# Softmax weights applied after the value product, and values, phi(keys) and retrieved values turned by VectorE and DMA instead of TensorE

## The chip, the core and the metric

The kernel runs on one core of a Trainium2 chip. Its engines each work through a queue of their own, in order: TensorE (PE in the profile; PEld is its weight load), VectorE (DVE), ScalarE (ACT), GpSimd (POOL) and SyncE (SP), which issues nearly all DMAs here. An instruction that waits holds up what stands behind it on its engine, and a DMA that waits for an earlier one holds up every DMA behind it in the queue of SP. The metric is the device time of one launch in microseconds (us). Before the change it is 2301.6 us, the median of three runs (2299.87 to 2302.35).

## The reference

One transformer layer over 2048 tokens of width 1024. The first half is an attention with a compressive memory: 32 heads of width 32, the tokens in four segments of 512. The second half is a layer norm and an MLP of inner width 3584. In the attention, for every head and segment `s`:

```python
logits = einsum("qd,kd->qk", qs, ks) * scale + mask   # causal inside the segment
p      = softmax(logits)
a_dot  = p @ vs
a_mem  = (phi(qs) @ M) / (phi(qs) @ z + 1e-6)         # phi(t) = t+1 if t>0 else exp(t)
o      = g * a_mem + (1 - g) * a_dot                  # g = sigmoid(beta), one number a head
M, z   = M + phi(ks).T @ vs,  z + sum(phi(ks))
```

Then `h = x + o @ wo`, and `h + MLP(LN(LN(h)))`. All is float32. The matrix products of the kernel split an operand into a high and a low part (`fp32r`) and add three products.

## The kernel before

The four segments are taken in two halves of two. In each half come an attention stage (about 40 to 500 us and 885 to 1375 us), the product with `wo`, and the MLP stages. Only the attention and its edges are touched by the change.

**Units.** Eight groups `g` of four heads times the two segments of the half make 16 units in a half, 32 in all. In half 0 they are segments 0 and 1, in half 1 segments 2 and 3. `dense` computes keys, queries and values of one unit: eight steps each for `kps`, `qps` and `vps`, three 128x512 matmuls a step, with the result laid out as 128 rows (4 heads x 32) by 512 tokens. Meanwhile `heads` runs the softmax of the unit before it, one step of `heads` after one step of `dense` (`interleave`).

**A head's pipeline.** `slot` runs six steps for a head after the list `PLAN`. In it three heads are under way: the current one (`q`: logits, row minimum, exponential), the one before (`n`: normalise; `t`: turn the weights so that keys lie on partitions; `s`: their low part) and the one before that (`a`: product with the values; `o`: into the output tile `ot`). Before the change `norm` multiplies all weights, 128 rows by up to 512, by the inverse of their row sum and by `1 - g`. It does so on POOL, after one reciprocal on DVE (L554, L557).

**What is turned.** Three things come with head dimensions on partitions and are needed with tokens on partitions, or the other way. These are the values (`vt` into `vn`, L469), phi of the keys (`pk` into `pkn`, L453; not in the last segment, which updates no memory), and what is retrieved from the memory (`om` into `pom`, L516; not in the first segment, which has none). Each is four 128x128 transposes on PE, with `ident` as the moving operand. ACT then writes the high part, or the copy, and DVE the low part.

**Late work.** The generator `late` of a unit is run during the next `dense`. It turns the values, queues small matmuls (`pm`: retrieval; `pmm`: memory update), which go out one at a time between the heads' matmuls (`one_small`), and turns what was retrieved.

**The queue of SP.** In each unit it carries 12 DMAs of 64 KB that stack keys (`ks`, L377), 12 that stack queries (`qs`, L377), the output tile to memory (`o_dram`, L609) and the loads of the next weights (`wr`, L326). The next unit's logits wait for `ks` and `qs`. A scheduler sets the order on each engine; only the instructions of some later stages are held to the order written.

**After the attention.** The last unit's heads run beside the first `wo` blocks (`wo_first`), which take the tiles `zx_tile(.., 3)` of the pool `zt` for a part of the weights.

Of the kernel before, what the change touches and what calls it, by code (L numbers as in the profile page):

```python
# [17 lines left out]
P = 128  # L18
S = 2048
# [11 lines left out]
PLAN = ('q1 S2', 'q0 n0 a0', 'q2 t0 a1', 'q3 n2 s0 o', 't1', 's1 t2')  # L31
# [12 lines left out]
def build(tc, x, wq, wk, wv, wo, beta, w1, b1, w2, b2, out):  # L44
# [39 lines left out]

    acts = {}
# [258 lines left out]
    def attention(half, first):  # L344
# [6 lines left out]

        def tmpr(name):
            return ab.tile([P, 512], F32R, tag="tmpr", name=name, bufs=6)
# [48 lines left out]
        def dense(g, sl, ws, u):  # L402
# [30 lines left out]
            for c in project(ws["v"], sl, "vps", vps):  # L433
# [16 lines left out]
                if c == 1 and s < 3:  # L450
                    pkn = ps_dense("pkn")
                    for i in range(4):
                        nc.tensor.transpose(pkn[:, i * P:(i + 1) * P], pk[:, i * P:(i + 1) * P], ident)  # L453
# [12 lines left out]
            def late():  # L466
                vn = ps_dense("vn")
                for c in range(4):
                    nc.tensor.transpose(vn[:, c * P:(c + 1) * P], vt[:, c * P:(c + 1) * P], ident)  # L469
                vn3 = vn.rearrange("p (a b) -> p a b", b=DH)  # L470
                nc.scalar.copy(vs[:, :, 0:32], vn3)
                nc.vector.tensor_tensor(vs[:, :, 32:64], vn3, raw(vs[:, :, 0:32]), op=ALU.subtract)
                yield
                if s > 0:
# [14 lines left out]
                    for i2 in range(2):  # L489
                        smalls("pm", [(lambda ps, ii=ii: ps[:, 256 * ii:256 * ii + 132],  # L490
                                       pqh[:, (2 * i2 + ii) * P:(2 * i2 + ii + 1) * P],
                                       pql[:, (2 * i2 + ii) * P:(2 * i2 + ii + 1) * P], mzh, mzl, True, True)
                                      for ii in range(2)], partial(memory, i2))
                left = len(small)
                if s < 3:
                    def update(pmm):
# [9 lines left out]
                                    vs[:, 4 * c:4 * c + 4, 0:32], vs[:, 4 * c:4 * c + 4, 32:64], c == 0, c == 3)  # L506
# [5 lines left out]
                if s > 0:  # L512
                    pom = ps_dense("pom")
                    for i in range(4):
                        one_small()
                        nc.tensor.transpose(pom[:, i * P:(i + 1) * P], om[:, i * P:(i + 1) * P], ident)  # L516
                    if s == 3:
                        yield
                        while acts["pth"][0] < 2:
                            yield  # L520
                    op = nc.scalar.copy(omt, pom)
                    if s == 3:
                        tc.add_manual_dep(op.ins, acts["pth"][1].ins.name, NOSYNC, reason="program order")
# [9 lines left out]
        def qk(st, i):  # L533
            u, j = st["u"], st["j"]
            if "pr" not in st:
                st["pr"] = ab.tile([P, 1280], F32, name="pr", bufs=2)
                st["mx"] = ab.tile([P, 32], F32, name="mx", bufs=4)
                st["nm"] = ab.tile([P, 32], F32, name="nm", bufs=4)
# [13 lines left out]
        def norm(st, i):  # L552
            pr, mx, nm, j, g = st["pr"], st["mx"], st["nm"], st["j"], st["u"]["g"]
            nc.vector.reciprocal(nm[:, 4 + i:6 + i], mx[:, 4 + i:6 + i])  # L554
            for k in (i, i + 1):
                pi = pr[:, offs[k]:offs[k] + P * (k + 1)]
                nc.gpsimd.tensor_scalar(pi, pi, nm[:, 4 + k:5 + k], gate[:, 1, 4 * g + j:4 * g + j + 1],  # L557
                                        op0=ALU.mult, op1=ALU.mult)
# [23 lines left out]
        def av(st, n):  # L582
# [4 lines left out]
            for jk in (0, 1) if n == 0 else (3, 2):  # L587
                w = 512 - P * jk
                v = u["vs"][:, 4 * jk + j, :]
# [10 lines left out]
        def av_out(st):  # L600
# [4 lines left out]
            if j == 3:  # L605
                if u["omt"] is not None:
                    nc.gpsimd.tensor_tensor(ot, ot, u["omt"], op=ALU.add)
# [8 lines left out]
        def slot(cur):  # L616
# [6 lines left out]
            ops = {"q": (cur, qk), "n": (cur, norm), "N": (p1, norm), "t": (p1, ptr), "s": (p1, sub), "S": (p2, sub),  # L623
# [820 lines left out]
```

## Time and profile before

| what | value |
|---|---|
| median of the runs | 2301.6 us |
| profiled execution, first to last instruction | 2296.2 us |
| granted TensorE clock | 1.000 |
| PE busy | 2270.4 us (99%) |
| PEld busy | 1890.8 us (82%) |
| DVE busy | 1540.3 us (67%) |
| ACT busy | 1225.0 us (53%) |
| POOL busy | 1092.4 us (48%) |

The page gives for each engine the time in which it was busy. A matmul's duration includes its way through the array, so consecutive matmuls overlap: what one costs in an unbroken run is the distance from its start to the next start, its pitch, and not its duration. Groups of instructions are listed by line and tile, with their count and mean duration, and waits are put down to the instruction that released them. For a DMA there are two numbers: how long SP was busy issuing it, and the time from its issue until its data had landed.

### The profile page before, as it was taken

The numbers are of one execution on the slowest core, as the hardware profiler recorded it, in microseconds if no ns is written. First come the engines' busy times: TensorE is split into PE (matmuls) and PEld (weight loads), VectorE is DVE, ScalarE is ACT, GpSimd is POOL, SyncE is SP. The second block draws the span as 40 slices with busy tenths as digits, with TensorE's granted clock in tenths as the row PEclk, the third lists the DMA queues.
The fourth block names the chain that finished last, engine by engine and source line by source line (L and its number), as shares of the span: only waits on it lengthen the run. The fifth ranks groups of instructions, "written<-read, shape, count | busy, mean of one in ns | idle before, by whom it ended". The sixth has DMA issues, their size and how long they took to land.

```text
span 2296.2 us, 35279 instructions
## 1 busy us (share of the span) xinstructions
PE 2270.4 (99%) x11769; PEld 1890.8 (82%) x11769; DVE 1540.3 (67%) x3173; ACT 1225.0 (53%) x2549; POOL 1092.4 (48%) x1134
## 2 busy tenths in 40 slices
PE   8999999999999999999999999999999999999999
PEld 6888888878888888888888887888888888888887
DVE  6777777776655565777777777565566766577563
ACT  6777777775453445777777776363344223322221
POOL 5545555555244442555555556253445554155430
PEclk9999999999999999999999999999999999999999
DMA  6333333345465654433333344466667976476762
GB/s 190 92 85 91 93 89 85 87 120 182 139 204 172 188 165 142 113 91 86 85 87 88 87 111 140 156 211 175 176 188 263 345 243 216 159 253 221 249 234 90
DMA packets 322719, 355.36 MB, mean 155 GB/s; under 512 B 26190, under 2 KB 218730, under 8 KB 322538
## 3 DMA queue, kind: packets, MB, share of 16 engines
q1 hardware_dynamic: 259370, 316.40, 45.4%
q10 hardware_dynamic: 63168, 36.71, 5.3%
q8 instruction: 93, 1.52, 0.3%
q14 instruction: 88, 0.72, 0.1%
HBM read 226.59 MB, written 76.09 MB: 132 GB/s over the span
## 4 chain that ended last, share of the span: by engine, by line
PE 91%; ACT 3%; POOL 2%; DVE 2%; issue 1%; DMA 1%; ACTq 0%; SPq 0%; POOLq 0%; DVEq 0%
PE po L1278 22%; PE bps L882 9%; PE cps L882 7%; PE dps L882 6%; PE po L593 6%; PE ppt L573 6%; PE pqk L541 3%; PE vps L116 2%; PE vps L115 2%; PE kps L115 2%; PE kps L116 2%; PE vps L117 2%; PE kps L117 2%; PE pwo L117 2%; PE pwo L116 2%; PE pwo L115 2%
## 5 line engine op out<-in xcount | busy, mean ns | idle before, releaser
L557 POOL TENSOR_SCALAR pr<-pr,nm,gate 128x128 f32<-128x128 f32 (+3 forms) x512 | 322.6, 639 | 345.9 <-DVE nm L554 260.0
L550 ACT ACTIVATE pr<-pr,mx 128x256 f32<-128x256 f32 (+3 forms) x512 | 287.6, 562 | 161.9 <-DVE mx L542 158.2
L580 DVE TENSOR_TENSOR ptl<-ppt,pth 128x512 fp32r<-128x512 f32 (+1 forms) x384 | 227.2, 599 | 86.2 <-ACT pth L575 82.0
L542 DVE CUSTOM_DVE_ANT_0 pr<-pqk,mask 128x256 f32<-128x256 f32 (+3 forms) x512 | 243.3, 484 | 46.5 <-PE pqk L541 43.7
L573 PE MATMUL ppt<-ident,pr 128*128 128x128 f32 x1280 | 223.6, 277 | 2.1 <-POOL pr L557 1.4
L575 ACT CAST pth<-ppt 128x512 fp32r<-128x512 f32 (+1 forms) x384 | 194.2, 517 | 39.0 <-PE ppt L573 33.1
L1288 DVE TENSOR_TENSOR c<-c,po 128x512 f32<-128x512 f32 x160 | 105.4, 683 | 143.1 <-PE po L1278 135.5
L573 PEld LDWEIGHTS ppt<-ident,pr 128*128 128x128 f32 x1280 | 164.6, 140 | 32.5 <-POOL pr L557 2.6
L541 PE MATMUL pqk<-ks,qs 96*128 96x256 f32 (+3 forms) x512 | 161.3, 315 | 0.0
L92 POOL TENSOR_TENSOR wl<-wr,wh 128x1024 fp32r<-128x1024 f32 x52 | 124.5, 2393 | 70.8 <-PE pqk L541 27.6
L593 PE MATMUL po<-pth,vs 128*64 128x512 f32 (+3 forms) x512 | 155.4, 326 | 0.3 <-ACT pth L575 0.2
L593 PE MATMUL po<-ptl,vs 128*64 128x512 f32 (+3 forms) x512 | 153.9, 310 | 1.3 <-DVE ptl L580 1.2
L1278 PE MATMUL po<-w2h,zh 128*128 128x512 f32 x378 | 121.1, 390 | 0.8 <-DVE zh L1218 0.4
L1135 POOL TENSOR_TENSOR w2r<-w2r 128x512 f32<-128x512 f32 x54 | 85.4, 1593 | 72.0 <-DVE c L1288 36.9
L541 PEld LDWEIGHTS pqk<-ks,qs 96*128 96x128 f32 x512 | 96.2, 188 | 21.5
L994 POOL TENSOR_TENSOR s<-r 128x512 f32<-128x512 f32 x28 | 43.6, 1559 | 143.4 <-DVE sa L1010 87.1
L882 PE MATMUL bps<-zh,sb 128*128 128x512 f32 x336 | 111.0, 391 | 0.0
L882 PE MATMUL bps<-zh,sa 128*128 128x512 f32 x336 | 110.8, 390 | 0.0
L115 PE MATMUL vps<-yh,wh 128*128 128x512 f32 x256 | 109.4, 427 | 0.9 <-DVE MZ L497 0.9
L115 PE MATMUL kps<-yh,wh 128*128 128x512 f32 (+1 forms) x264 | 110.1, 417 | 0.0
L115 PE MATMUL qps<-yh,wh 128*128 128x512 f32 x256 | 106.8, 417 | 0.0
L1278 PE MATMUL po<-w2h,hl 128*128 128x512 f32 x322 | 103.2, 390 | 0.5 <-POOL hl L1218 0.3
(241 smaller groups left out, 6657.1 us busy)
## 6 DMA issues: line engine op xcount, KB each, us to landing
hr<-h_dram SPq DMA_DIRECT2D x112, 448.0 KB, 5.4
w2r<-in_B_w SPq DMA_DIRECT2D x122, 256.0 KB, 4.4
r<-in_B_w SPq DMA_DIRECT2D x56, 512.0 KB, 4.5
h_dram<-ht ACTq DMA_DIRECT2D x84, 256.0 KB, 3.7
ks<-kh SPq DMA_DIRECT2D x256, 64.0 KB, 2.0
qs<-qh SPq DMA_DIRECT2D x256, 64.0 KB, 2.0
wr<-in_A_wo SPq DMA_DIRECT2D x32, 512.0 KB, 4.0
wx<-in_B_w SPq DMA_DIRECT2D x56, 256.0 KB, 3.5
```

Of the source, the lines that this page charges most:

```text
L115: nc.tensor.matmul(ps, ah, bh, start=first, stop=False)
L116: nc.tensor.matmul(ps, ah, bl, start=False, stop=False)
L541: nc.tensor.matmul(pqk[:, :n], u["qs"][j][:, i * P:(i + 1) * P], u["ks"][j][:, 0:n], start=True, stop=True)
L542: nc.vector.tensor_tensor_reduce(out=st["pr"][:, offs[i]:offs[i] + n], in0=pqk[:, :n], in1=mask[:, 512 - n:512], op0=ALU.add, op1=ALU.min, ...
L550: nc.scalar.activation(pi, pi, AF.Exp, bias=mx[:, i:i + 1], scale=-1.0, accum_out=mx[:, 4 + i:5 + i])
L557: nc.gpsimd.tensor_scalar(pi, pi, nm[:, 4 + k:5 + k], gate[:, 1, 4 * g + j:4 * g + j + 1], op0=ALU.mult, op1=ALU.mult)
L573: nc.tensor.transpose(ppt[:, o:o + P], pr[:, offs[i] + jk * P:offs[i] + (jk + 1) * P], ident)
L575: acts["pth"] = n, nc.scalar.copy(pth[:, base:base + w], ppt[:, :w])
L580: nc.vector.tensor_tensor(o, x0, x1, op=ALU.subtract)
L593: nc.tensor.matmul(po[:, P * jk:], v, st[part][:, koff[jk]:koff[jk] + w], start=(jk, part) == (0, "pth"), stop=(jk, part) == (2, "ptl"))
L882: nc.tensor.matmul(ps, x_[:, c, :], y_[:, c, :], start=first and c == 0 and n == 0, stop=last and c == 3 and n == 2, skip_group_check=True)
L1278: nc.tensor.matmul(ps, x_[:, k], y_[k], start=opens and k == 0 and i == 0, stop=closes and k == self.KP - 1 and i == 2, skip_group_check=True)
```

## The change

The softmax weights are no longer normalised before they are turned. `norm` and its tiles are gone. `inverse` takes the four row sums of a head at once into a tile `rs`; after the fourth head POOL multiplies them by `1 - g`. `weigh` turns this 128x16 tile with one transpose on PE, copies it, writes it to memory and reads it back with each row repeated over the 32 partitions of its head. The result `w` multiplies the whole output tile on POOL in `av_out`.

The three turns leave PE. `turned` transposes 32x32 blocks on DVE, writes the tile to memory, and reads it back with four DMAs, one for each 32 partitions. So keys and tokens inside a unit come in another order, and the operands of `pmm`, `av` and `av_out` are indexed to fit. The values' halves (`vs`) are now made in `late` after the retrieval's matmuls are queued and six more steps have passed. The low part of phi(keys) moves from DVE to POOL.

```diff
-PLAN = ('q1 S2', 'q0 n0 a0', 'q2 t0 a1', 'q3 n2 s0 o', 't1', 's1 t2')
+PLAN = ('q1 r S2', 'q0 a0', 'q2 t0 w a1', 'q3 s0 o', 't1', 's1 t2')
...
+        scr = [acts["zt"].tile([P, 4, 512], F32, tag=f"t{x_}3", name=f"sc{x_}") for x_ in "hl"]
+        def turned(src, to, mid):
+            nc.vector.transpose(mid.rearrange("p (c k d) -> p c k d", c=4, k=4), src.rearrange("p (k c d) -> p c k d", c=4, k=4))
+            d = turn_dram[acts.get("turned", 0) % len(turn_dram)]
+            acts["turned"] = acts.get("turned", 0) + 1
+            nc.sync.dma_start(d, mid)
+            for c in range(4):
+                nc.sync.dma_start(to[32 * c:32 * c + 32].rearrange("j (h x) -> j h x", h=4),
+                                  d[:, c * P:(c + 1) * P].rearrange("(h j) x -> j h x", h=4))
...
+                if c == 3 and s < 3:
+                    kn = scr[1][:, 2 + sl]
+                    turned(pk, kn, scr[1][:, 0])
...
-                    pkn = ps_dense("pkn")
-                    for i in range(4):
-                        nc.tensor.transpose(pkn[:, i * P:(i + 1) * P], pk[:, i * P:(i + 1) * P], ident)
-                    nc.scalar.copy(pkh, pkn)
-                if c == 2 and s < 3:
-                    nc.vector.tensor_tensor(pkl, pkn, raw(pkh), op=ALU.subtract)
+                    pkn = kn.rearrange("p (h k d) -> p k h d", h=4, k=4)
+                    nc.scalar.copy(pk4[0], pkn)
+                if c == 3 and s < 3:
+                    nc.gpsimd.tensor_tensor(pk4[1], pkn, raw(pk4[0]), op=ALU.subtract)
...
-            vt = tmp("vt")
-            nc.scalar.copy(vt, vps)
+            vn = scr[0][:, 2 + sl]
+            turned(vps, vn, scr[0][:, 0])
...
-                vn = ps_dense("vn")
-                for c in range(4):
-                    nc.tensor.transpose(vn[:, c * P:(c + 1) * P], vt[:, c * P:(c + 1) * P], ident)
-                vn3 = vn.rearrange("p (a b) -> p a b", b=DH)
-                nc.scalar.copy(vs[:, :, 0:32], vn3)
-                nc.vector.tensor_tensor(vs[:, :, 32:64], vn3, raw(vs[:, :, 0:32]), op=ALU.subtract)
-                yield
...
+                for _ in range(6):
+                    yield
+                vn3 = vn.rearrange("p (a b) -> p a b", b=DH)
+                nc.scalar.copy(vs[:, :, 0:32], vn3)
+                yield
+                nc.vector.tensor_tensor(vs[:, :, 32:64], vn3, raw(vs[:, :, 0:32]), op=ALU.subtract)
...
-                    pom = ps_dense("pom")
-                    for i in range(4):
-                        one_small()
-                        nc.tensor.transpose(pom[:, i * P:(i + 1) * P], om[:, i * P:(i + 1) * P], ident)
...
-                    op = nc.scalar.copy(omt, pom)
+                    turned(om, omt, tmp("omx"))
...
-        def norm(st, i):
-            nc.vector.reciprocal(nm[:, 4 + i:6 + i], mx[:, 4 + i:6 + i])
-            for k in (i, i + 1):
-                nc.gpsimd.tensor_scalar(pi, pi, nm[:, 4 + k:5 + k], gate[:, 1, 4 * g + j:4 * g + j + 1],
-                                        op0=ALU.mult, op1=ALU.mult)
+        def inverse(st):
+            nc.vector.reciprocal(rs[:, 4 * j:4 * j + 4], st["mx"][:, 4:8])
+            if j == 3:
+                nc.gpsimd.tensor_tensor(r4, r4, gate[:, 1, 4 * u["g"]:4 * u["g"] + 4].unsqueeze(2).to_broadcast([P, 4, 4]),
+                                        op=ALU.mult)
+        def weigh(st):
+            if j < 3:
+                return
+            w = u["w"] = tmp("w") if u["g"] == NG - 1 and u["s"] % 2 else scr[n][:, 1]
+            pw = ps_dense("pw")
+            nc.tensor.transpose(pw[0:16, 0:P], u["rs"][:, 0:16], ident)
+            nc.scalar.copy(w[0:16, 0:P], pw[0:16, 0:P])
+            nc.sync.dma_start(d, w[0:16, 0:P])
+            nc.sync.dma_start(w, bass.AP(tensor=d.tensor, offset=d.offset, ap=[[512, 4], [0, DH], [1, 512]]))
...
             if j == 3:
+                nc.gpsimd.tensor_tensor(ot, ot, u["w"], op=ALU.mult)
```

More of the change, by code (lines that the diff above doesn't have):

```diff
@@ L83, in build @@
     h_dram = [[dram.tile([S // P, P, FB // 4, P], F32, name=f"h_dram{i}{s}") for s in range(2)] for i in range(2)]
+    turn_dram = [dram.tile([P, 512], F32, name=f"turn_dram{k}") for k in range(6)]
+    r_dram = [dram.tile([16, P], F32, name=f"r_dram{k}") for k in range(2)]
     acts = {}
@@ L512, in late @@
                 if s > 0:
-                    pom = ps_dense("pom")
-                    for i in range(4):
-                        one_small()
[L516 to L523, printed above, removed]
+                    turned(om, omt, tmp("omx"))
                 while small:
@@ L550, in soft @@
             nc.scalar.activation(pi, pi, AF.Exp, bias=mx[:, i:i + 1], scale=-1.0, accum_out=mx[:, 4 + i:5 + i])
-        def norm(st, i):
-            pr, mx, nm, j, g = st["pr"], st["mx"], st["nm"], st["j"], st["u"]["g"]
-            nc.vector.reciprocal(nm[:, 4 + i:6 + i], mx[:, 4 + i:6 + i])
-            for k in (i, i + 1):
-                pi = pr[:, offs[k]:offs[k] + P * (k + 1)]
-                nc.gpsimd.tensor_scalar(pi, pi, nm[:, 4 + k:5 + k], gate[:, 1, 4 * g + j:4 * g + j + 1],
-                                        op0=ALU.mult, op1=ALU.mult)
+        def inverse(st):
+            u, j = st["u"], st["j"]
+            if j == 0:
+                u["rs"] = ab.tile([P, P], F32, name="rs", bufs=1)
+            rs = u["rs"]
+            nc.vector.reciprocal(rs[:, 4 * j:4 * j + 4], st["mx"][:, 4:8])
+            if j == 3:
+                r4 = rs[:, 0:16].rearrange("p (h i) -> p h i", i=4)
+                nc.gpsimd.tensor_tensor(r4, r4, gate[:, 1, 4 * u["g"]:4 * u["g"] + 4].unsqueeze(2).to_broadcast([P, 4, 4]),
+                                        op=ALU.mult)
+        def weigh(st):
+            u, j = st["u"], st["j"]
+            if j < 3:
+                return
+            n = acts["weighed"] = 1 - acts.get("weighed", 0)
+            w = u["w"] = tmp("w") if u["g"] == NG - 1 and u["s"] % 2 else scr[n][:, 1]
+            pw = ps_dense("pw")
+            nc.tensor.transpose(pw[0:16, 0:P], u["rs"][:, 0:16], ident)
+            nc.scalar.copy(w[0:16, 0:P], pw[0:16, 0:P])
+            d = r_dram[n]
+            nc.sync.dma_start(d, w[0:16, 0:P])
+            nc.sync.dma_start(w, bass.AP(tensor=d.tensor, offset=d.offset, ap=[[512, 4], [0, DH], [1, 512]]))
         def ptr(st, n):
@@ L605, in av_out @@
             if j == 3:
+                nc.gpsimd.tensor_tensor(ot, ot, u["w"], op=ALU.mult)
                 if u["omt"] is not None:
-                    nc.gpsimd.tensor_tensor(ot, ot, u["omt"], op=ALU.add)
+                    ot4 = ot.rearrange("p (k c j) -> p k c j", k=4, c=4)
+                    nc.gpsimd.tensor_tensor(ot4, ot4, u["omt"].rearrange("p (c k j) -> p k c j", k=4, c=4), op=ALU.add)
                 if u["g"] < NG - 1:
@@ L621, in call @@
                     fn(st, *args)
-            ops = {"q": (cur, qk), "n": (cur, norm), "N": (p1, norm), "t": (p1, ptr), "s": (p1, sub), "S": (p2, sub),
+            ops = {"q": (cur, qk), "r": (p1, inverse), "w": (p1, weigh), "t": (p1, ptr), "s": (p1, sub), "S": (p2, sub),
                    "a": (p2, av), "o": (p2, av_out)}
```

11 lines of the change are left out of this document (7 added, 4 removed).

## The prediction

> **What bounds the kernel now.** I read the totals and the chain of waits first, then busy time by stretch of the attention, then what PE itself waited for.
>
> ```profile
> span 2296.2 us, 35279 instructions
> ...
> PE 2270.4 (99%) x11769; PEld 1890.8 (82%) x11769; DVE 1540.3 (67%) x3173; ACT 1225.0 (53%) x2549; POOL 1092.4 (48%) x1134
> ...
> PE 91%; ACT 3%; POOL 2%; DVE 2%; issue 1%; DMA 1%; ACTq 0%; SPq 0%; POOLq 0%; DVEq 0%
> ```
>
> ```profile
> core 0: us, PE busy (x) PEld busy (x) DVE busy (x) ACT busy (x) POOL busy (x), PEclk, DMA share, GB/s
> 40.00:490.00 450.00, 448.42 (x2722) 378.99 (x2722) 334.68 (x989) 326.28 (x830) 234.91 (x330) 1.00 0.36 93
> 490.00:520.00 30.00, 26.71 (x160) 21.41 (x159) 23.00 (x63) 22.75 (x54) 19.46 (x22) 1.00 0.53 158
> ...
> 940.00:1360.00 420.00, 419.25 (x2563) 355.32 (x2562) 318.55 (x948) 309.67 (x783) 234.83 (x313) 1.00 0.35 88
> 1360.00:1390.00 30.00, 27.56 (x159) 21.59 (x158) 22.57 (x66) 23.49 (x57) 18.98 (x22) 1.00 0.48 145
> ```
>
> PE is the bound: 91% of the chain is its own work, and inside the attention it is idle for 1.6 of 450 us and 0.8 of 420 us. The full clock was granted (1.00). Only at the two edges, where the last heads run beside the first `wo` blocks, is PE idle, 3.3 and 2.4 us of 30. The next busiest engines there are DVE, 334.68/450 = 74%, and ACT, 73%. So a transpose taken off PE shortens the attention by its pitch, as long as nothing else comes late.
>
> **What the removed transposes cost.**
>
> ```profile
> L469 PE MATMUL vn<-ident,vt x128: 271/272/329, 40.6 to 1380.8; 128*128 128x128 f32 x128
> ...
> L453 PE MATMUL pkn<-ident,pk x96: 270/272/273, 31.5 to 1333.3; 128*128 128x128 f32 x96
> ...
> L516 PE MATMUL pom<-ident,om x96: 270/296/331, 80.5 to 1387.9; 128*128 128x128 f32 x96
> ```
>
> ```profile
> 309.21 0.34 PE L541 MATMUL pqk<-ks,qs 96*128 96x384 f32 x1
> 309.39 0.60 PE L573 MATMUL ppt<-ident,pr 128*128 128x128 f32 x4
> ...
> 316.24 0.60 PE L469 MATMUL vn<-ident,vt 128*128 128x128 f32 x4
> 316.60 0.43 PE L541 MATMUL pqk<-ks,qs 96*128 96x384 f32 x1
> 316.86 0.60 PE L573 MATMUL ppt<-ident,pr 128*128 128x128 f32 x4
> ```
>
> There are 128 + 96 + 96 = 320 transposes, 80 groups of four. One lasts 272 ns, but they overlap: four start at 316.24 and the next matmul at 316.60, 0.36 us. That matmul then takes 0.26 us to the next start, against 0.18 for the same one at 309.21, so the group costs 0.44 us, 0.11 a transpose. Removed: 80 x 0.44 = 35.2 us. Added: one `pw` transpose a unit, 32 x 0.11 = 3.5 us. Net on PE: -31.7 us. Nothing covers it, PE being the path.
>
> The Trainium skill (TensorE: Matmul & The Clock Gate, Part 4: PE-mode transpose) gives about 275 ns for a transpose in one kernel's context. The 272 ns above agree as a duration; taken as the cost, it is the third rival below.
>
> **The other engines.**
>
> ```profile
> L557 POOL TENSOR_SCALAR pr<-pr,nm,gate 128x128 f32<-128x128 f32 (+3 forms) x512 | 322.6, 639 | 345.9 <-DVE nm L554 260.0 <-PE qps L117 37.2 <-PE vps L117 13.2
> ...
> L554 DVE RECIPROCAL nm<-mx 128x2 f32<-128x2 f32 x256 | 42.0, 164 | 86.2 <-ACT pr L550 85.6
> ...
> L607 POOL TENSOR_TENSOR ot<-ot,omt 128x512 f32<-128x512 f32 x24 | 30.9, 1287 | 27.4 <-DVE ot L604 27.4
> ...
> L472 DVE TENSOR_TENSOR vs<-vn,vs 128x512 fp32r<-128x512 f32 x32 | 22.0, 686 | 0.7 <-ACT vs L471 0.4 <-DMA qs<-qh 0.3
> ...
> L521 ACT COPY omt<-pom x24: 562/586/608, 83.4 to 1388.3; 128x512 f32<-128x512 f32 x24
> ...
> L1010 DVE TENSOR_TENSOR sa<-s,sa 128x512 fp32r<-128x512 f32 x56 | 52.5, 974 | 32.7 <-ACT sa L1009 32.7
> ```
>
> POOL loses `norm`, 322.6 us, and gains 32 output multiplications and 24 low parts at 1.29 (L607's row): 72 us, and 32 small ones. ACT loses the copies of `vt` and `omt` (56 at 0.59 us, L521's row) and gains 32 of a 16x128 tile. DVE loses half of 42.0 us of reciprocals and 24 low parts (16 us). It gains 80 block transposes of 128x512, and `vs` reads SBUF in place of PSUM. No block transpose is in this trace: 0.69 us (L472) and 0.97 us (L1010, SBUF sources) bound it; I take 0.8, nearer the first since it has one source. That is 64 us, and 32 x 0.29 = 9 us for `vs`; net +36 us over two attention stages, which takes DVE from 74% to 79%. None of these is on the path: PE waits for neither engine now, and the exponentials are ready for their turn earlier by one POOL pass. If the 79% were bunched, the low parts `ptl` would be late first, and PE's `po` behind them.
>
> **The queue of SP, worked through.** Each turn is five DMAs and each weighing two, all in the one queue that also stacks `ks` and `qs`.
>
> ```profile
> 313.08 0.48 PE L115 MATMUL kps<-yh,wh 128*128 128x512 f32 x1
> ...
> 345.08 0.48 PE L115 MATMUL kps<-yh,wh 128*128 128x512 f32 x1
> ...
> 345.85 0.28 PE L541 MATMUL pqk<-ks,qs 96*128 96x256 f32 x1
> ...
> 1125.10 0.48 PE L115 MATMUL kps<-yh,wh 128*128 128x512 f32 x1
> ...
> 1155.75 0.48 PE L115 MATMUL kps<-yh,wh 128*128 128x512 f32 x1
> ```
>
> ```profile
> 323.44 0.51 SPq L377 DMA_DIRECT2D ks<-kh  x1
> ...
> 329.40 0.53 SPq L609 DMA_DIRECT2D o_dram<-ot  x1
> 335.82 0.51 SPq L377 DMA_DIRECT2D ks<-kh  x1
> ...
> 337.72 1.17 SPq L377 DMA_DIRECT2D qs<-qh  x2
> ...
> 343.36 1.22 SPq L377 DMA_DIRECT2D qs<-qh  x2
> ...
> 1143.38 0.34 SPq L609 DMA_DIRECT2D o_dram<-ot  x1
> ```
>
> ```profile
> q1 hardware_dynamic: 259370, 316.40, 45.4%
> ...
> ks<-kh SPq DMA_DIRECT2D x256, 64.0 KB, 2.0
> ...
> wr<-in_A_wk SPq DMA_DIRECT2D x16, 512.0 KB, 4.4
> ...
> o_dram<-ot SPq DMA_DIRECT2D x28, 256.0 KB, 2.3
> orr<-o_dram SPq DMA_DIRECT2D x28, 256.0 KB, 3.2
> ```
>
> ```profile
> L609 SPq DMA_DIRECT2D o_dram<-ot x28: 332/463/527, 81.8 to 1359.5; - x28
> ...
> L326 SPq DMA_DIRECT2D wr<-in_A_wk x15: 368/528/954, 22.8 to 1249.2; - x15
> ```
>
> This is the dense of a segment-0 unit, 345.08 - 313.08 = 32.0 us long, with retrieval and update of the unit before beside it; the PE saving makes it 30.8 (three groups out, one `pw` in). Times below count from its start. Nine `ks` go out from 10.4 to 16.2, `o_dram` at 16.3, the last three `ks` at 22.7, twelve `qs` from 24.6 to 32.1, 0.63 us a DMA. In the changed program's SP queue stand, after `o_dram`: the write of the keys, the write of the retrieval, a weight load, three key reads, the three `ks`, a key read, four retrieval reads, then `qs`. Reads and writes that touch memory take 0.46 to 0.53 us to issue (two rows above); I use 0.5, with 0.95, the longest `wr`, as the other end. The multiplication by `w` puts `o_dram` at 17.6. Key write 18.1; it lands at 18.1 + 2.3 = 20.4, behind the other two issues. Three reads to 21.9; `ks` when their buffer is free, about 22.2, to 24.1; five reads to 26.6; `qs` from 26.6 to 34.2. The first head's three are issued by 28.5 and land by about 30. Its first logits stood 0.77 us after the next dense began (345.85); in the changed PE order they come after two key steps of 0.7 and one `po` of 0.23, at 30.8 + 1.65 = 32.4. Margin 2.4 us.
>
> The last key read lands at 26.6. ACT's copy of it stands after the exponentials of the last head's first two blocks, about 26, and `pth` behind it waits up to 1 us; PE needs that bank again three steps, some 3.5 us, later. Values: write at 34.2, landed 36.5, reads to 38.5, landed 40.5, which is 9.7 in the next dense, where ACT takes them at about 13 (after `kh` and three steps). `w` is issued at 38.5 and lands by 42 (`orr`, 3.2), 11 in the next dense; the output tile wants it at 16.
>
> The other dense of half 0 turns no retrieval, so it has more room. In half 1 the dense that turns both has only 1155.75 - 1125.10 = 30.65 us, 29.4 after the change, and its `o_dram` stood at 18.3, with the addition before it; the multiplication makes that 19.6. The same sum, 2 us later from there on but without the weight load, lands the first `qs` at about 30.3. The changed PE order puts the logits that use them behind three key steps and the `po` of a head, at 29.4 + 3.0 = 32.4. Margin 2.1 us. So for the inner stretch I take 0 us lost. At 0.95 us an issue the eight or nine reads and writes ahead of `qs` add 0.45 each, about 4 us, 2 beyond the margin, in each of the 16 such dense steps: 32 us is the other end. A gain below 0 has no source in this queue.
>
> **The edges.** `w` and the turned tiles live in the very tiles that `wo_first` takes for its fourth weight block, so that block's split now waits until the last values are halved and the next-to-last unit is weighed. That is about 16 us after the last `vps` (where `o_dram` stood), then about 1 us ACT and 2.4 us POOL. PE reaches it after 12 `wo` steps (8.4 us) and what heads can run, and heads alone are held by ACT. The idle of 3.3 and 2.4 us I let grow by 2.5 each: +5 us, between 0 and the 10 us of an edge in which PE loses a third of its 30 us twice.
>
> **Sum.** 2296.2 - 31.7 + 0 + 5 = 2269.5 us of span. The runs' median lies 2301.6 - 2296.2 = 5.4 above this execution's span: 2274.9, say 2275.
>
> **Rivals.**
> 1. SP late (slower). In a dense that turns both, SP issues 24 DMAs at 0.63 us and some 19 at 0.5, 25 us of 29 to 31, and it stands still for four landings. The price: 31.7 - 5 = 26.7 us are gained, so a stall of 1.7 us in each of 16 such dense steps cancels it. With issues of 0.95 and landings of 3.2 in place of 2.3 the stall is 2 to 4 us: at 3 us, 2275 + 16 x 3 = 2323, from 2307 to 2339. For it: only 4 to 6 us of 30 are free, and each wait delays all behind it. Against: the margins of 2 us above, and the issues' median of 0.46 to 0.53. One more way into it, to which I give 0.02 of its chance, is the read of `w`: its source is four rows, each repeated. If only four DMA engines carry it, each moves 64 KB at 316.40 MB / (0.454 x 16 x 2296.2 us) = 19 GB/s, 3.4 us more. Then it lands at 14.5 in place of 11, 1.5 us before the output tile wants it, and the `ks` behind it share the four. The Trainium skill (DMA: Bandwidth & Descriptors, Rules for kernel authors) says that an outermost dimension below 16 confines a DMA to at most that many engines; by that rule this is what happens, and no run here shows it yet.
> 2. The edges take more: 10 us each in place of 2.5 gives 2290. For it: heads alone are bound by ACT. Against: only two edges.
> 3. The transposes cost their full 272 ns: 320 x 0.272 - 32 x 0.272 = 78 us, 2301.6 - 78 + 5 = 2228. Against: the starts above.
>
> That the transposes stay on PE is excluded: the changed PE queue holds none of the three groups.
>
> **How the numbers follow.** The forecast, with edges of 0 to 5 us each and small stalls (2266 to 2286): 0.54. Rival 2, or small stalls at SP (2286 to 2297): 0.17. Rival 3: 0.02. Gains and stalls that cancel (2297 to 2306): 0.06. Rival 1: 0.21, half of it above 2316. Faster 0.73, same 0.06, slower 0.21, where 0.2%, 4.6 us, is about what a measurement of this kernel can tell from no change. The range from 2264 to 2316 leaves out rival 3, half of rival 1 and some 0.04 of the forecast's lower end; the forecast's own range is 2266 to 2286.
>
> **What would show it.** Right: 288 PE instructions fewer; pairs of dense steps of about 60 us in place of 61.9; PE idle below 3 us in each attention stage; more idle at 490 to 520. Wrong at SP: PE's `pqk` or `kps` waiting for `qs`. Wrong at ACT or DVE: `po` waiting for `pth` or `ptl`, with the copies of `scr` late behind a DMA. Wrong at the pitch: attention shorter by 78 us.

## The result and the profile after

The changed kernel takes 2378.9 us (median of 4 runs, 2376.0 to 2383.7) against 2301.7 us before: 1.034 times as long, 95% interval 1.032 to 1.035. The forecast was 2275 us, with 2264 to 2316 as the range. It failed in direction and in size.

The totals of the profile after, then busy time by stretch (the columns are those of the stretches before):

```profile
span 2377.0 us, 34795 instructions
...
PE 2273.8 (96%) x11481; PEld 1865.3 (78%) x11481; DVE 1574.1 (66%) x3101; ACT 1193.8 (50%) x2525; POOL 868.1 (37%) x710
```

```profile
40.00:490.00 450.00, 415.76 (x2399) 339.93 (x2398) 328.26 (x887) 291.82 (x762) 130.70 (x129) 0.99 0.49 132
...
940.00:1360.00 420.00, 398.86 (x2302) 324.42 (x2301) 306.44 (x858) 278.67 (x719) 129.09 (x127) 1.00 0.52 138
```

The 288 instructions are gone from PE (11769 to 11481), but PE now stands idle for 34 of 450 us and 21 of 420, where it was idle for 1.6 and 0.8. Every other engine is less busy there too (DVE 334.68 to 328.26 us of 450). So no engine became the bound: PE waits. Its waits in the whole program, as the view of waits gives them, who waited for whom, us in total, times, longest:

```profile
PE ppt L596 <- DVE ptl L603: 15.5, 17, 1.5
PE pwo L118 <- POOL zl L94: 15.2, 2, 8.5
PE po L616 <- DVE ptl L603: 14.6, 14, 1.6
PE pmm L409 <- DVE vs L508: 11.8, 14, 1.7
PE pt L270 <- ACT xt L260: 10.0, 2, 8.2
PE pm L409 <- ACT scl L578: 7.6, 12, 0.7
PE pm L409 <- POOL pql L466: 4.6, 4, 2.0
PE pm L409 <- ACT sch L578: 4.0, 7, 0.6
```

Only the wait for `xt` was there before at this size (9.2 us). The new ones are for the low halves of the weights `ptl`, for those of the values `vs`, for the copy of `pw` (written into `scl` or `sch`), and, once an attention stage, for a weight block of `wo`.

The granted clock differs too: 1.000 before, 0.992 to 0.994 in the four runs after. In six stretches of 3.4 to 10.2 us, 30.6 us in all, it was half; the kernel before has none in the attention or at its edges. One of them begins as PE has waited 1.6 us for `ptl`:

```profile
197.20:200.60 3.40, 3.37 (x13) 2.98 (x14) 1.43 (x7) 1.23 (x5) 0.00 (x0) 0.50 0.44 101
```

```profile
198.04 0.63 PE L118 MATMUL vps<-yl,wh 128*128 128x512 f32 x1
198.47 0.63 PE L119 MATMUL vps<-yh,wl 128*128 128x512 f32 x1
...
200.90 0.40 PE L118 MATMUL vps<-yl,wh 128*128 128x512 f32 x1
201.13 0.40 PE L119 MATMUL vps<-yh,wl 128*128 128x512 f32 x1
```

The distance from one start to the next is 0.43 us in it and 0.23 right behind it. PE is busy for 22 us of the six stretches, so by an estimate from these numbers half clock costs some 11 us. PE's idle time in the whole program grew by 77 us (25.8 to 103.2). No run shows what lowers the clock.

Where in time the 81 us between the two profiled executions (2296.2 and 2377.0) lie is read from the starts of the first and last dense step of each attention stage (first `kps` matmul) and the last `pwo` matmul. In half 0 the count begins with the second dense step, at about 38 us. Rows for the experiments stand beside them (differences in us; some tenths uncertain):

| kernel | time | half 0, first to last dense | last dense to last `pwo` | half 1, first to last dense | last dense to last `pwo` |
|---|---|---|---|---|---|
| before | 2301.6 | 430.7 | 146.0 | 451.1 | 145.1 |
| after | 2378.9 | 463.8 | 159.1 | 469.5 | 160.1 |
| weighing alone | 2321.6 | 430.1 | 153.7 | 453.1 | 158.5 |
| weighing, not the last group | 2305.4 | 430.0 | 149.8 | 451.7 | 147.0 |
| after, values by PE early | 2323.7 | 437.3 | 157.0 | 448.8 | 154.6 |
| after, values by PE late | 2339.7 | 435.3 | 156.5 | 462.4 | 159.0 |
| retrieved values alone turned | 2297.7 | 428.4 | 145.5 | 449.9 | 148.8 |

After: +33 us in half 0, +18 in half 1, +13 and +15 at the two edges. The stages between are unchanged to about 1 us.

What a stall looks like, in one dense step of half 0 (start, duration, engine, and in brackets the idle time before and its releaser):

```profile
303.12 0.48 PE L117 MATMUL kps<-yh,wh 128*128 128x512 f32 x1
...
318.52 1.28 POOL L629 TENSOR_TENSOR ot<-ot,sch 128x512 f32<-128x512 f32 x1 [2.32 <-DVE ot L627]
319.02 1.32 DVE L508 TENSOR_TENSOR vs<-sch,vs 128x512 fp32r<-128x512 f32 x1
320.40 0.33 PE L409 MATMUL pmm<-vs,pkh 128*128 128x128 f32 x1 [1.39 <-DVE vs L508]
...
327.94 2.38 POOL L94 TENSOR_TENSOR wl<-wr,wh 128x1024 fp32r<-128x1024 f32 x1
329.00 1.88 DVE L383 SCALAR_TENSOR_TENSOR pq<-e,r 128x512 f32<-128x512 f32 x1 [0.72 <-ACT r L378]
330.80 0.68 DVE L603 TENSOR_TENSOR ptl<-ppt,pth 128x512 fp32r<-128x512 f32 x1
331.53 0.39 PE L616 MATMUL po<-ptl,vs 128*64 128x384 f32 x1 [1.64 <-DVE ptl L603]
...
336.31 0.48 PE L117 MATMUL kps<-yh,wh 128*128 128x512 f32 x1
...
368.86 0.48 PE L117 MATMUL kps<-yh,wh 128*128 128x512 f32 x1
```

Two things happen. The memory update `pmm` stands right behind the low halves of the values, and PE waits 1.39 us for them. Nine us later phi of the queries, `pq`, takes 1.88 us on DVE beside POOL's pass over the weights; `ptl` stands behind it in DVE's queue, and PE's `po` waits 1.64 us. The step that begins at 303.12 lasts 33.2 us, and the pair of steps from there to 368.86 takes 65.7 us (64 to 67 in all pairs of half 0), where 61.9 was before and about 60 was forecast.

### The profile page after: what moved, and what is told of

It is laid out like the page before. It is cut to its first block, busy times and chain, and to the rows that moved or that the text cites. A ratio compares the mean times of both kernels' runs of the same rounds, so it can differ in the third digit from the quotient of the medians.

```text
span 2377.0 us, 34795 instructions
## 1 busy us (share of the span) xinstructions
PE 2273.8 (96%) x11481; PEld 1865.3 (78%) x11481; DVE 1574.1 (66%) x3101; ACT 1193.8 (50%) x2525; POOL 868.1 (37%) x710
## 5 line engine op out<-in xcount | busy, mean ns | idle before, releaser
L596 PE MATMUL ppt<-ident,pr 128*128 128x128 f32 x1280 | 223.9, 278 | 15.5 <-DVE ptl L603 15.5
L598 ACT CAST pth<-ppt 128x512 fp32r<-128x512 f32 (+1 forms) x384 | 186.0, 512 | 40.1 <-PE ppt L596 35.2
L616 PE MATMUL po<-ptl,vs 128*64 128x512 f32 (+3 forms) x512 | 156.7, 313 | 14.9 <-DVE ptl L603 14.6
L119 PE MATMUL qps<-yh,wl 128*128 128x512 f32 x256 | 101.6, 397 | 1.3 <-POOL wl L94 1.3
L118 PE MATMUL kps<-yl,wh 128*128 128x512 f32 (+1 forms) x264 | 102.5, 388 | 0.1
```

The lines of the kernel that those rows point to most:

```text
L596: nc.tensor.transpose(ppt[:, o:o + P], pr[:, offs[i] + jk * P:offs[i] + (jk + 1) * P], ident)
L598: acts["pth"] = n, nc.scalar.copy(pth[:, base:base + w], ppt[:, :w])
```

## Experiments

The theories at the start: the turns lose the time (values arriving late, with DVE's queue behind them), or the weighing does (a new order of steps, a PSUM bank for `pw`, the shared tiles). Each time is to be read against 2301.6 before and 2378.9 after.

**The two parts alone.** The weighing alone is the kernel before with

```
-PLAN = ('q1 S2', 'q0 n0 a0', 'q2 t0 a1', 'q3 n2 s0 o', 't1', 's1 t2')
+PLAN = ('q1 r S2', 'q0 a0', 'q2 t0 w a1', 'q3 s0 o', 't1', 's1 t2')
+  inverse, weigh, ot * w, as in the change; no turned()
```

> The weighing alone (inverse sums, w, no normalising pass), with values, keys and retrieved values still transposed by TensorE at their old places. After is 104 us above the 2275 us that I forecast. If the weighing and its new order of steps lose them (the reciprocal in VectorE's queue behind an exponential, a dense PSUM bank for pw, the shared edges), this kernel takes 2380 to 2410. If the turns lose them, it takes 2301.6 + 3.5 for 32 pw + 5 to 15 at the edges = 2310 to 2320.

The turns alone are the changed kernel with `norm` and the old `PLAN` put back.

> The turns alone, with GpSimd's normalising pass and the old order of steps. If the turns lose the time (TensorE waiting for vs and ptl, which stand late in VectorE's queue), 2350 to 2385. If the weighing loses it, 2301.6 - 35.2 + 5 = 2271, up to 2285.

Measured: 2321.6 and 2371.9 us. The turns carry most of it. The weighing alone leaves the pace of the attention as it was (table) and loses 20 us, all at the edges.

**The bank of `pw`.**

```
-            pw = ps_dense("pw")
+            pw = psum.tile([P, 512], F32, tag="pt", name="pw", bufs=2)
```

> The changed kernel with pw in one of the two banks of the ppt tiles instead of one of the three dense banks. PE's pm waited 11.6 us for pw's copy. If that bank costs what the wait shows, 2367; if it is only a place where another lateness surfaces, 2375 to 2383; if the ppt tiles miss their bank, above 2385.

Measured: 2378.7, no difference. The waits for `pw`'s copy are gone, and this row has grown from 15.5 us:

```profile
PE ppt L596 <- DVE ptl L603: 19.4, 17, 1.6
```

The bank is a place where lateness shows, not its source.

**Values through PE again.**

```
-            vn = scr[0][:, 2 + sl]
-            turned(vps, vn, scr[0][:, 0])
+            vt = tmp("vt")
+            nc.scalar.copy(vt, vps)
     late():
+                vn = ps_dense("vn")    # four transposes, halves, first thing, as before
```

> The changed kernel with the values alone back on TensorE (copy, four transposes, halves at the start of the next dense, update of the memory early), keys and retrieved values still turned by VectorE and DMA. TensorE gets 32 x 0.44 = 14 us of work back. If the late halves of the values are the main loss (pmm and the low parts behind them in VectorE's queue), 2320 to 2350; if not, 2379 + 14 = 2393.

Measured: 2323.7, 55 us less than after although PE does 14 us more. Of the three turns, that of the values costs by far the most. The run changes two things, the way of the values and the place of their halves; they are told apart further down.

**Values' halves earlier, or the update later.** The first kernel has the six steps ahead of the halves cut to three and the two behind them made five; the second keeps six and has five behind.

```
-                for _ in range(6):
+                for _ in range(3):     # second kernel: 6
...
-                yield
-                yield
+                for _ in range(5):
+                    yield
```

> The changed kernel with the copy of the values' upper halves and the subtraction of the lower halves three steps of the dense loop earlier, the update of the memory (pmm) where it stands. If pmm loses its time because the lower halves stand too near ahead of it, its 11.8 us of waits go, with what follows them: 2345 to 2367. If the loss sits in VectorE's queue wherever the halves stand (long SBUF operations beside GpSimd, low parts of the probabilities behind them), 2370 to 2385.

> The changed kernel with the memory update (pmm) queued three steps of the dense loop later, the halves of the values where they stand. In each dense step with a retrieval PE's pmm waits 1.4 to 1.8 us for the lower halves, and a step of qps takes 3.6 us. If that wait is paid once and nothing takes its place, 12 of them a half are worth 24 x 1.6 = 38 us: 2340. If MZ, behind pmm, then comes later to GpSimd and moves its pass over the weights further into phi of the queries, the loss moves there: 2370 to 2390.

Measured: 2381.4 and 2356.7. Asking for the halves earlier did nothing, because they did not come earlier: the scheduler put the subtraction where it was, 15.9 us into a dense step of half 0 with a retrieval in both traces, with the update right behind it and GpSimd's pass beside it in most of these steps. So this run does not test earlier halves. PE waited as before:

```profile
PE pmm L409 <- DVE vs L508: 10.6, 14, 1.4
```

Moving the update away from them gave 22 us, of the 38 expected. Part of the wait came back at `po`, which also reads `vs` (8.3 us, 7 times). Nor are the 22 us the update's alone: in this run `pq` moved away from GpSimd's pass as well, and fell from 1613 to 763 ns on average in half 0.

**GpSimd beside VectorE.** Is `pq` long because of the pass beside it? One kernel takes the pass away from the changed kernel. The matmuls with the weights' low halves read the upper halves after the first group, so these count twice in the output; count and shape of the matmuls are the same.

```
+        if not low:                    # g > 0
+            nc.vector.tensor_copy(wh, wr)
+            return wh, wh
```

> The changed kernel without GpSimd's pass over the weights' lower halves after the first group: the matmuls read the upper halves in their place (same count and shapes; the result is then that of rounded weights). In the profile of the changed kernel phi of the queries (pq) takes 1.88 us on VectorE beside that pass and about 0.69 without, and PE's po waits 1.6 us behind it. If GpSimd beside VectorE is what makes pq long, pq falls to about 0.7 to 1.0 us and the time by 12 to 16 dense steps x 2 halves x 1 to 2 us, to 2330 to 2355. If pq is long for another reason, 2372 to 2380.

The other adds such a pass where there was none, in the kernel that only weighs:

```
+                        for _ in range(2):
+                            nc.gpsimd.tensor_tensor(scr[0][:, 0], qparts[0], qparts[1], op=ALU.subtract)
                         pq = phi_sum(qparts, "pq")
```

> The weighing alone (pq 0.686 us there, 2321.6 us) with two idle subtractions of 128x512 added on GpSimd that start when phi of the queries does (2.6 us of GpSimd work, 24 times, output unused). If GpSimd's passes stretch VectorE's SBUF operations beside them, pq takes 1.3 to 1.9 us, and the time grows by up to 24 x 1.5 = 36 us, 2325 to 2355. If not, pq stays at 0.69 and the time at 2318 to 2325.

Measured: 2357.2 and 2323.1. The group of `pq` on DVE in 40 to 490 us (busy, then mean ns of one): before, after, without the pass, weighing alone, weighing with the added passes.

```profile
L369 DVE SCALAR_TENSOR_TENSOR pq<-e,r 128x512 f32<-128x512 f32 x7 | 6.8, 965 | 0.0
```

```profile
L383 DVE SCALAR_TENSOR_TENSOR pq<-e,r 128x512 f32<-128x512 f32 x7 | 11.3, 1613 | 3.8 <-ACT r L378 3.6
```

```profile
L386 DVE SCALAR_TENSOR_TENSOR pq<-e,r 128x512 f32<-128x512 f32 x7 | 4.8, 684 | 0.2
```

```profile
L372 DVE SCALAR_TENSOR_TENSOR pq<-e,r 128x512 f32<-128x512 f32 x7 | 4.8, 686 | 0.0
```

```profile
L372 DVE SCALAR_TENSOR_TENSOR pq<-e,r 128x512 f32<-128x512 f32 x7 | 12.7, 1808 | 0.0
```

The effect on `pq` is shown in both directions. Its price depends on the slack behind it. In the changed kernel the removal of the pass gives 22 us, all in half 0 (463.8 to 442.1 from first to last dense; half 1 stays at 470). It also shortens other DVE work there, the low halves of the values (967 to 775 ns) and the cast of the weights (910 to 717 ns), so the 22 us are the price of the pass and not of `pq` alone. In the kernel that only weighs, the same 1.1 us on DVE cost 0.4 us a pair of steps, and the whole run is within 2 us: `pq` grew as expected and the time did not.

**The edges.** First the shared tile was taken away from the kernel that only weighs:

```
-            w = u["w"] = tmp("w") if u["g"] == NG - 1 and u["s"] % 2 else scr[n][:, 1]
+            w = u["w"] = tmp("w") if u["g"] == NG - 1 else scr[n][:, 1]
```

> The weighing alone as in the earlier run of it, but w of both last units in a tmp tile, so that no tile shared with the wo stage is in use at the end of the attention. The weighing alone took 2321.6. Its attention ran at the pace of before, its two edges had 5.2 and 9.7 us less TensorE work done than before. If the shared tile is the cause, 2301.6 + 3.5 = 2302 to 2307; if the edges are slow for another reason (the new order of steps), 2317 to 2323.

Then the weighing of the last group was (`norm` runs for `g == NG - 1`, `inverse`, `weigh` and the multiplication for the others):

```
+            if g < NG - 1:
+                return                 # in norm; the reverse in inverse and weigh
```

> The weighing alone, but the last group of each half normalised as before (GpSimd's pass), so that its two output tiles wait for no w. The weighing alone took 2321.6, 21 us of it lost between the last dense step of each half and the end of the wo stage. If the weighing of the last units is what is slow there (w by DMA, multiplication, then ACT and VectorE in their queues), 2302 to 2307. If not, 2315 to 2322.

Measured: 2320.5 and 2305.4. The shared tile that the prediction priced is indeed waited for; in the kernel that only weighs:

```profile
523.03 0.79 PE L117 MATMUL pwo<-zl,oh 128*128 128x512 f32 x1 [4.12 <-POOL zl L93]
```

With `w` in a tile of its own the loss stays, by another way. `w` comes 8 us after SP issued its read, POOL's multiplication waits for it, ACT's and DVE's split of the output tile stands in their queues behind that, and the other unit's `pth` behind the split:

```profile
514.31 0.58 SPq L576 DMA_DIRECT2D w<-r_dram  x1
...
522.35 1.26 POOL L624 TENSOR_TENSOR ot<-ot,w 128x512 f32<-128x512 f32 x1 [4.05 <-DMA w<-r_dram]
...
525.64 0.39 PE L611 MATMUL po<-pth,vs 128*64 128x384 f32 x1 [3.28 <-ACT pth L593]
```

Normalising the last group as before gives 16 us. What stays, 3.8 us, is about the price of 28 `pw` (3.1). Not all of the 16 us are waiting. In the kernel that only weighs PE is busy for 14 us at half clock, all at the edges, worth about 7 us; without the weighing of the last group it is 3.4 us, worth about 2.

**One turn alone.** The kernel before with only the retrieved values turned (`turned(om, omt, tmp("omx"))` for the four `pom` transposes), and with only the keys turned.

> The kernel before with the retrieved values alone turned by VectorE and DMA, 24 of the 80 groups. If a group is worth its 0.44 us on TensorE and nothing comes late, 2301.6 - 10.6 = 2291. If a group is worth its four durations, 2301.6 - 24 x 1.17 = 2274. If VectorE's extra 0.7 us and the DMAs eat it, 2298 to 2310.

> The kernel before with the keys alone turned by VectorE and DMA, 24 of the 80 groups; the low part goes to GpSimd as in the change. If nothing comes late, 2301.6 - 10.6 = 2291. If ACT's copy behind the DMA or VectorE's block transpose holds up the low parts of the probabilities, 2300 to 2320.

Measured: 2297.7 (ratio 0.998, 0.997 to 0.999) and 2304.9 (1.001, 1.000 to 1.002). The first beats the kernel before, by 0.2%. Here the price of a group can be read where it vanishes. Between two steps of `vps` stood four `pkn` transposes before; with the keys turned, all else in that step is the same:

```profile
366.62 0.48 PE L115 MATMUL vps<-yh,wh 128*128 128x512 f32 x1
...
367.40 0.60 PE L453 MATMUL pkn<-ident,pk 128*128 128x128 f32 x4
...
367.97 0.48 PE L115 MATMUL vps<-yh,wh 128*128 128x512 f32 x1
```

```profile
367.20 0.48 PE L116 MATMUL vps<-yh,wh 128*128 128x512 f32 x1
...
368.12 0.48 PE L116 MATMUL vps<-yh,wh 128*128 128x512 f32 x1
```

1.35 against 0.92: 0.43 us a group, the 0.44 of the forecast. Yet the two kernels give 4 us and -3 us in place of 10.6 each. With the retrieved values turned, the edge of half 1 grew by 3.7 us (table), and 6 us of PE's work stand there at half clock, worth about 3. Where the turn of the keys alone loses (5 us between the dense steps of half 1, 4 us at the edge of half 0) was not followed up.

**Late place or new way, and do the causes add?** Values by PE, but at the late place of the change; the three causes (update, pass beside `pq`, last group) removed together; and the values-by-PE kernel with the last group normalised, with the keys turned in both halves and in half 1 only.

```
     late(): after the retrieval's small matmuls
                 for _ in range(6):
                     yield
+                vn = ps_dense("vn")    # four transposes, halves
```

> The changed kernel with the values transposed by TensorE, but where the change puts their halves: after the retrieval's small matmuls and six more steps, the update behind them. With the transposes and halves at their old early place the kernel took 2323.7. If the late place is what costs, 2355 to 2390 here. If VectorE's block transpose and the DMAs cost, 2320 to 2330.

> The changed kernel with three causes removed at once: the memory update three steps later, no GpSimd pass over the weights' lower halves after the first group (upper halves used in their place), the last group normalised as before. If the causes add, 2379 - 22 - 22 - 16 to 20 = 2315 to 2320. If they are one stall seen from three sides, 2335 to 2357. If nothing else were lost, 2275.

> The changed kernel with values by TensorE at the old place and the last group normalised as before; keys and retrieved values turned. From 2323.7 less the 16 us that the last group gave in the kernel that only weighs: 2305 to 2310. Of the transposes removed, 48 groups less 28 pw are worth 18 us on TensorE, so 2284 if nothing were lost in half 0.

> The same with the keys of half 0 transposed by TensorE as before, so that half 0 turns only what it retrieves. In the run with keys turned half 0 lost 6.6 us and half 1 gained 2.3; the run with retrieved values alone gained 2.3 in half 0. If the keys' turn is what half 0 loses by, 2295 to 2300; if the weighing does, 2304 to 2310.

Measured: 2339.7, 2330.5, 2310.9, 2302.9. The late place costs 16 us, 14 of them in half 1 (448.8 to 462.4), and the way through DVE and DMA another 39. What the late place brings in PE's waits is the retrieval, which now goes out first and waits for the bank of `pw`; these two waits are not in the kernel with the values by PE early. No run moves `pw` to another bank in this kernel, so this cause is read from the waits and not tested:

```profile
PE pm L409 <- ACT scl L580: 9.2, 13, 0.7
...
PE pm L409 <- ACT sch L580: 5.3, 7, 0.8
```

No wait of the update for `vs` is among PE's waits in this run: in a dense step of half 0 with a retrieval the subtraction starts 12.5 us into the step and the update at 14.5. In the changed kernel the subtraction starts at 15.9, reads SBUF, takes up to 1.6 us beside GpSimd's pass, and the update waits for it (11.8 us).

The three causes removed singly give 22, 22 and 16 us (the last in the kernel that only weighs; with the values by PE it is 13, 2323.7 to 2310.9), together 48, so they overlap. In the kernel without the three the matmuls with the weights' low halves again read the upper ones. It still stands 55 us above the forecast, with these waits first among those of the attention:

```profile
PE ppt L611 <- DVE ptl L618: 16.5, 23, 1.2
...
PE pm L412 <- ACT scl L593: 9.6, 14, 0.7
...
PE po L631 <- DVE ptl L618: 4.7, 8, 1.5
```

Turning the keys in half 0 costs 8 us (2310.9 against 2302.9) where 16 groups should give 7. That loss is in the trace of the kernel with both halves' keys turned, in the dense step that begins at 285.65:

```profile
285.65 0.40 PE L117 MATMUL kps<-yh,wh 128*128 128x512 f32 x1
...
314.07 0.62 ACT L471 CAST pkh<-scl 128x512 fp32r<-128x512 f32 x1 [1.33 <-DMA scl<-turn_dram]
...
315.71 0.57 ACT L608 CAST pth<-ppt 128x512 fp32r<-128x512 f32 x1
...
316.32 0.69 DVE L613 TENSOR_TENSOR ptl<-ppt,pth 128x512 fp32r<-128x512 f32 x1 [1.83 <-ACT pth L608]
...
317.15 0.41 PE L606 MATMUL ppt<-ident,pr 128*128 128x128 f32 x2 [1.57 <-DVE ptl L613]
```

The turned keys come 28.4 us into the step; ACT waits for them with `pth` behind it, and PE pays.

**The added work without the waiting.** The values-by-PE kernel with the values' turn added, its outcome unused, and with the block transpose alone:

```
+            turned(vps, scr[0][:, 2 + sl], scr[0][:, 0])
```

> Values by TensorE at the early place (2323.7 us), and the values' turn by VectorE and its five DMAs added as well, with nobody reading the outcome. If the work itself costs (VectorE's queue, SP's queue, memory traffic beside VectorE), 2335 to 2365. If only the waiting for it costs, 2322 to 2328.

> The same with the block transpose alone, without the DMAs. If VectorE's 32 x 0.71 = 23 us are what costs, the same time as with the DMAs, 2335 to 2350. If the DMAs are what costs, 2322 to 2328 here and more with them.

Measured: 2332.2 and 2324.2, against 2323.7. The 32 block transposes, 23 us of DVE, cost nothing measurable; the DMAs cost 8 us, of which about 5 are paid at half clock (PE busy for 22 us at half clock against 12). The other 31 of the 39 us are a remainder and were not measured by themselves. They come with the use of the outcome: the halves are then made from SBUF and meet GpSimd's pass, and `pmm` and `ptl` wait behind them.

## Why the prediction was wrong

A ladder, each rung measured, with what the forecast gave for it:

| from, to | measured | forecast's terms |
|---|---|---|
| before, weighing without the last group | 2301.6 to 2305.4: +3.8 | 28 `pw` x 0.11: +3.1 |
| last group weighed as well | to 2321.6: +16.2 | part of the edges' +5 |
| keys and retrieved values turned | to 2323.7: +2.1 | 48 x 0.44: -21.1 |
| values' halves late, still by PE | to 2339.7: +16.0 | 0 |
| values by DVE and DMA | to 2378.9: +39.2 | 32 x 0.44: -14.1 |

Point by point:

- **Removed transposes, 0.44 us a group: right** as a price (0.43 at the place where a group vanishes). It is a saving on PE's own work only. The net of 31.7 us was there to be had, and the kernel became 77 us slower, so some 109 us of new loss stand against it. PE's idle time grew by 77 us of this, and half clock costs about 11; the other 20 were not separated. The instruction count was right, and the third rival (the full 272 ns) is out.
- **"None of these is on the path: PE waits for neither engine now": the step that failed.** It added up busy time by engine, found DVE at 79%, and gave the case "`ptl` would be late first, and PE's `po` behind them" no price. That is what the trace shows, with DVE at 73%: PE waits 30 us for `ptl` (15.5 at `ppt`, 14.6 at `po`) and 12 us for the values' low halves, where before it waited 1.6 us for `ptl`, and the inner stretch for which 0 us were taken lost 33 and 18 us. What counts is which instruction stands ahead of `ptl` when it is wanted: `pq` at 1.88 us, or an ACT queue that holds `pth` behind the copy of turned keys.
- **POOL was booked as relieved.** Its passes that stayed moved, the weights' pass in half 0 further into `pq` (965 ns on average before, 1613 after), and there they stop DVE. The prediction took 0.8 us for the block transpose (0.71 measured, and free). It took +0.29 for `vs`, for reading SBUF, and the average in half 0 rose by 0.28:

```profile
L508 DVE TENSOR_TENSOR vs<-sch,vs 128x512 fp32r<-128x512 f32 x14 | 13.5, 967 | 0.0
```

  That agreement is luck. Of these 14, those that run free of a pass take 0.68 to 0.69 us, as from PSUM before; the average is raised by those beside a pass, 1.15 to 1.63 us.
- **The late place of the values' halves was not priced at all.** The prediction asked whether the data arrive in time, and not what PE does right behind them. The retrieval `pm`, which now goes out first, meets `pw`'s bank, and the update `pmm` follows the halves at once. It costs 16 us even with PE transposes, with 14.5 us of waits at the bank, and half clock costs about 5 us more than at the early place.
- **SP's queue: right** in that PE's waits show none for `qs`, and the first rival is not what happened, although the result lies on its side. The landing of the turned keys was put at 26.6 us into the step, with "up to 1 us" on ACT and no effect on PE. In the run with values by PE it was 28.4, 1.3 us on ACT and 1.6 on PE; that costs 8 us over half 0.
- **The edges: +5 in the sum, +28 measured.** The mechanism named, the shared tiles, is there, but it is one of two, and without it the other costs as much (2320.5 against 2321.6). The other, the last units' multiplication in front of a split in ACT's and DVE's queues, was not seen. With `w` in a tile of its own POOL still waited 4 us for it. Of the 28 us half clock costs about 6.
- **The range** went up to 2316 because only SP's queue was allowed to lose much. Each of the two largest rungs alone would have taken the result out of the forecast's own range.

What stays open: after the three causes are taken away some 55 us remain against the forecast. PE's waits for `ptl`, for `pw`'s copy and for `pql` hold most of what is seen of them; the 8 us of DMA work are likely among them, half clock costs some 3 us, and the rest was not separated. Nor was the read of `w` from four rows, to which the first rival gave a small part: its 8 us, in the run with a tile of its own, fell together with loads for `wo` in the same queue.

## What to carry to other kernels

That PE is 99% busy says that everything arrives in time; it does not say with how much to spare. Before taking work off PE by a longer way around, list for each moved result the instruction right behind it on every queue, and give each a price, because the saving is a sum and the waits come at single places. Sums of busy time by engine say nothing of this: 23 us of extra DVE work were free, while the weights' pass beside `pq` cost 22 us. And try the parts singly: here one turn of three was worth keeping, for 0.2%.

## What the runs showed of the hardware

- A VectorE operation with two SBUF sources is held up by a GpSimd pass that began before it. In the kernel with the added passes:

```profile
371.77 2.99 POOL L442 TENSOR_TENSOR sch<-e,r 128x512 f32<-128x512 f32 x2 [1.09 <-ACT r L367]
...
371.80 1.81 DVE L372 SCALAR_TENSOR_TENSOR pq<-e,r 128x512 f32<-128x512 f32 x1
```

  GpSimd starts 0.03 us earlier; `pq` takes 1.81 in place of 0.69 us. The low halves of the values, once read from SBUF, are hit in the same way (0.65 to 0.69 us alone, 1.32 beside a pass). In the dense step shown after the change both end a little over half a microsecond behind the pass: `vs` at 320.34 behind 319.80, `pq` at 330.88 behind 330.32. The wait lies inside the duration of the VectorE row, so no idle time and no releaser is shown for it. Hit too is the cast of the weights, with one SBUF source (686 ns on average in the kernel that only weighs, 910 after). Operations that take one of their two sources from PSUM are not (`ptl` of 128x512: 681 ns on average after, 690 before). The Trainium skill (SBUF — State Buffer, SBUF: two separate sides) says that the pair of ports which the two engines share is an exclusive lock for a whole instruction, and counts VectorE operations with two SBUF inputs, or in a two-port mode, among those that need it. The runs agree, and by that rule the move of `vs` from a PSUM to an SBUF source, and any shift of GpSimd's passes, should have been priced in the forecast.
- A VectorE block transpose of 128x512 takes 0.67 to 0.72 us from PSUM or SBUF.
